# Softcap attention, gated MLP and gated convolution on one core: a new order for the first pairs, a bank moved, the last output in halves

## The chip, the core and the metric

The kernel runs on one core of a Trainium2 chip. Its metric is the device time of one execution in microseconds (us). Several runs are made, and their median counts. One further execution is recorded by the hardware profiler, and that recording is called the trace here.

The core has these engines: TensorE (PE, the matrix multiplies, with PEld for the loading of weights), VectorE (DVE), ScalarE (ACT), GpSimd (POOL) and SyncE (SP, which issues most of the DMAs). Each engine works through its own queue in order. An instruction that waits for a semaphore holds up all that stands behind it on that engine.

## The reference

Three stages follow each other, on 2 batches, 448 positions, 12 heads of 64 and a model width of 768:

```python
scores = scale * q @ k.T                       # per head
scores = cap * tanh(scores / cap)
attn = exp(scores - max); attn /= sum + 1e-9
x = attn @ v                                   # heads laid side by side: [2, 448, 768]

h = gelu(x @ w_in)                             # 768 -> 1024
u, v = h[..., :512], h[..., 512:]
v = layer_norm(v) * g_ln
x = x + (u * (w_sg @ v + b_sg)) @ w_out        # 512 -> 768

h = relu(x @ w2_in)                            # 768 -> 1024
y = (h * sigmoid(conv3(h))) @ w2_out           # 1024 -> 768, the output
```

## The kernel before

**Precision.** Most operands are kept as two parts, hi (rounded) and lo (the rest), and one product is three matmuls: hi by hi, hi by lo, lo by hi. `split` makes the two parts. The weights arrive as 64-bit floats, and `decode` turns each piece into hi and lo with a few ACT and DVE instructions (tiles `f`, `hd`, then `WI`, `WO` or `W`).

**Attention.** The heads are worked on in 12 pairs N, and each pair in two halves, so that the loop in `attention` runs over R = 2N + half. `scores(N, half)` writes scores to the tile `sc`, which takes four PSUM banks and exists once. So the next scores can start only when ACT has read the last ones (`tanh`, L403, into `raw`). ACT then runs `exp` on `raw` in place (L412). Pair 0 is an exception: its first scores go to the tile `pv` instead, and its `tanh` takes the scale `qscale` from a small tile `one`, which `constants` computes from the input `cap`. `one` also holds `guard`, the 1e-9 of the reference under the same shift as the sums.

`value` and `values` then multiply `raw` by the values (`V`, and `vlast` for the last 64 positions) and by ones, which gives the row sums; all this goes to `pv`. For half 0, DVE first adds two key blocks (`sm`, L459), and the sums use `sm`. On ACT `both` is copied to `E` when a pair is complete. Division follows many steps later: sums to `ss`, reciprocal, a round through DRAM to `rb`, then `E` times `rb`, split into `X`. The last pair divides at once through PE (`norm_pe`, with `sel`).

**What sets the order.** PE's order in the attention is written out: each matmul is pinned behind the last one (`ordered`, L386). On ACT and DVE, `pin` does the same for chosen instructions; what is not pinned is placed by a scheduler that plans ahead of the run. `later(k, fn)` puts work k ticks off, two ticks to a step R. SP issues its loads in one pinned order, each waiting for the load eight before it. `IDLE` and `WARM` are matmuls on zeros that keep PE at work.

**Behind the attention.** At R = 23 to 26 four units of the next stage (`FILL`, `mmw`) are computed between the last values. Three of them use the single bank `mo` of the pool `psm`; unit 1 uses a bank of the `sc` tile (`fi`). `gelu` reads such a bank twice, with ACT and DVE alternating, and ends in `u` (L230), which frees the bank. The gated MLP (`u_unit`, `v_unit`, `sg_unit`, `o_unit`) takes its banks by the function `bank`. The last stage ends with `f_unit`: ACT copies 128 by 448 results to `o`, and SP issues the store (L952, L953).

Of the kernel before, what the change touches and what calls it, by code (L numbers as in the profile page):

```python
# [19 lines left out]
P = 128  # L20
# [19 lines left out]

WARM = 15

K0 = 2 * P

IDLE = {0: (1, 4), 3: (3, 5)}

# [7 lines left out]
def stages(  # L54
# [19 lines left out]

    now = [0]
    lasta, lastv, lastr, lasts = [None], [None], [None], [None]

# [55 lines left out]

    heads = []

    def decode_half(hi, lo, src, pool, bufs, wait, hi_eng, top_eng):

        n = src.shape[1]
        r = pool.tile([P, 512, 2], U32, tag="f64", name="f64", bufs=bufs)[:, :n]
        words = r.rearrange("p c w -> p (c w)").bitcast(U16)  # L140
        sync(words[:, : 4 * n - 1], src.rearrange("r c w -> r (c w)").bitcast(U16)[:, 1:])
        low = r[:, :, 0]
        top = words.rearrange("p (c w) -> p c w", w=4)[:, :, 2].bitcast(BF16)
        heads.append(heads.pop(0))
        hd = heads[-1][:, :n]

        def s1():
            half = hd.bitcast(F16).rearrange("p (c w) -> p c w", w=2)[:, :, 1]
            with pin(lasta), pin(lastv):
                if top_eng == "a":  # L150
                    A.activation(half, top, AF.Copy)
                else:
                    V.tensor_copy(half, top)

        def s2():
            V.scalar_tensor_tensor(
                out=low, in0=low, scalar=13, in1=hd, op0=ALU.logical_shift_right, op1=ALU.bitwise_or
            )
            if hi_eng == "a":
                A.activation(hi, f(low), AF.Copy)  # L160
            else:
                V.tensor_copy(hi, f(low))

        def s3():
            V.tensor_tensor(out=lo, in0=f(low), in1=f(hi), op=ALU.subtract)

        for k, fn in zip(wait, (s1, s2, s3)):
            later(k, fn)
# [69 lines left out]
    def u_done(b, i, ps):  # L238
# [7 lines left out]
        later(1, s2b)  # L246

    def constants(pool):
        V.tensor_scalar(
            out=capc, in0=capt, scalar1=CAP_MAX, scalar2=-CAP_MAX, op0=ALU.min, op1=ALU.max  # L250
        )
        V.reciprocal(out=rcap, in_=capc if bounded else capt)
        V.tensor_scalar(
            out=qscale, in0=rcap, scalar1=1.0 / math.sqrt(D), scalar2=None, op0=ALU.mult
        )

        V.tensor_scalar(out=ncap, in0=capc, scalar1=-1.0, scalar2=None, op0=ALU.mult)
        V.tensor_tensor(out=ncap, in0=ncap, in1=capc, op=ALU.min)
        A.activation(guard, ncap, AF.Exp)
        if not bounded:  # L260
            V.tensor_scalar(out=guard, in0=guard, scalar1=1e-9, scalar2=None, op0=ALU.mult)
        heads[:] = [pool.tile([P, 512], U32, name=f"hd{i}") for i in range(2)]
# [12 lines left out]
    def attention(att, psa):  # L275
# [35 lines left out]
        def prep_q(n):  # L311
            qr, _ = qraw[n]
            q = Qt[n] = att.tile([P, 2, S], F32R, tag="Q", name="Q", bufs=2)
            if n == 0:

                A.activation(q[:, 0], qr, AF.Copy)
# [36 lines left out]
        if WARM:  # L353
# [4 lines left out]
            for i in range(WARM):  # L358
                T.matmul(wps, lhsT=wz[:, :P], rhs=wz, start=True, stop=True)  # L359
        constants(att)  # L360
        creg = A.alloc_register("creg")
        A.reg_load(creg, capc[0:1].bitcast(mybir.dt.int32))

# [7 lines left out]
        for t in range(4):  # L371
            G.memset(sel[t * 32 : t * 32 + 1, t], 1.0)
        prep_k(0, slice(0, K0))
        prep_q(0)
        with pin(lastv):
            prep_k(0, slice(K0, ST))
            V.tensor_scalar(out=guard, in0=guard, scalar1=1e-9, scalar2=None, op0=ALU.mult)

# [9 lines left out]

        late, sm0 = [], [None]
        sums = psa.tile([P, 3 * 512], F32, tag="pv", name="pv", bufs=1)  # L390

        def scores(N, half):

# [27 lines left out]
            for g in range(2 * half, 2 * half + 2):  # L421
# [23 lines left out]
                if N == 0 and g < 2:  # L445
                    soft(raw[:, 2 * g : 2 * g + 2], to[:, 2 * g : 2 * g + 2, :S])
                    if g:
                        expo(raw[:, 0:2])
                        expo(raw[:, 2:4])
                if R in IDLE and g == IDLE[R][0]:  # L450
                    for _ in range(IDLE[R][1]):
                        ordered(idle, lhsT=wz[:, :P], rhs=wz, start=True, stop=True)
            if half:
                soft(raw, ps)
            elif N:
                soft(raw, ps[:, :, :S])
            if half == 0:
                held[N] = att.tile([P, 2, S], F32, tag="sm", name="sm", bufs=2)
                sm = V.tensor_tensor(out=held[N], in0=raw[:, 0:2], in1=raw[:, 2:4], op=ALU.add)  # L459
                if N == 0:  # L460
                    sm0[0] = sm

# [119 lines left out]
        def norm_pe(N, both):  # L582

            b, p = divmod(N, NPAIR)
            both_e = att.tile([P, 2 * (S + HS)], F32, tag="E", name="E", bufs=3)[:, S + HS :]
            A.activation(both_e, both, AF.Copy)
            e, r = both_e[:, :S], both_e[:, S:]
            V.tensor_scalar(out=r, in0=r, scalar1=guard, scalar2=None, op0=ALU.add)
            V.reciprocal(out=r, in_=r)

# [16 lines left out]
        for R in range(2 * NN + LAGS[1] + 1):  # L607
            N, half = divmod(R, 2)
            if R == 23:
                columns(att)  # L610
            if R == 4:
                load_vlast(3, NN)
            for j, at in enumerate(WIN):
# [3 lines left out]
            if R < 2 * NN:  # L617
                if half == 0 and N + 2 < NN:
                    load(N + 2)
                if half == 0 and N + 1 < NN:  # L620
                    load_v(N + 1)
                if R == 1:

                    start_values(0)
                    scores(N, half)
                    value(0, 0)
                    value(0, 1)
                else:
                    scores(N, half)
                if R == 2:  # L630
                    values(0, 0, True)
                    done += 1
                if half == 0 and N + 1 < NN:
                    with pin(sm0) if N == 1 else ExitStack():
                        prep_q(N + 1)
                        prep_k(N + 1)
            if R in FILL:

                i, k0, k1 = FILL[R]
                if k0 == 0:  # L640
                    if i == 1:
                        free = psa.tile([P, 4, 512], F32, tag="sc", name="fi", bufs=1)
                    fill[i] = free[:, i, :S] if i == 1 else psm.tile([P, 512], F32, tag="mo", name="mo")[:, :S]
                for k in range(k0, k1):
# [3 lines left out]
            tick()  # L648
            if R > 1 and done < 2 * NN and R - done >= LAGS[R >= LAGS[2]]:
                values(*divmod(done, 2))  # L650
# [77 lines left out]
    def rest():  # L728
# [3 lines left out]
        with ExitStack() as s1:  # L732
# [18 lines left out]
            def bank(n):  # L751
                return (psm if n < 4 or n % 4 == 3 else ps1).tile([P, 512], F32, tag="mo", name="mo")

# [153 lines left out]
        with ExitStack() as s2, ExitStack() as last:  # L907
# [38 lines left out]
            def f_unit(b, m):  # L946
                ps = ps1.tile([P, 512], F32, tag="mo", name="mo")[:, :S]
                c = slice(m * P, (m + 1) * P)
                for i in range(NF):
                    mm3(ps, W2[:, 0, i, c], W2[:, 1, i, c], HG[:, 0, i, b], HG[:, 1, i, b], i == 0, i == NF - 1)  # L950
                o = c2.tile([P, S], F32, tag="cv", name="o", bufs=2)
                A.activation(o, ps, AF.Copy, scale=0.5)  # L952
                nc.sync.dma_start(outT[c, b * S : (b + 1) * S], o)  # L953
# [38 lines left out]
    if bounded:  # L992

        over = one[0:1, 7:8].bitcast(mybir.dt.int32)
        V.tensor_tensor(out=over, in0=capt[0:1], in1=capc[0:1], op=ALU.not_equal)
        flag = nc.values_load(over, min_val=0, max_val=1)
# [70 lines left out]
```

## Time and profile before

| what | value |
| --- | --- |
| median of 3 runs | 327.97 us (326.82 to 328.14) |
| the profiled execution | 327.65 us |
| its span, first to last instruction | 325.8 us |
| mean granted TensorE clock | 0.994 |
| PE busy | 316.0 us |
| PEld busy | 261.6 us |
| DVE busy | 242.7 us |
| ACT busy | 219.8 us |
| POOL busy | 36.7 us |
| DMA | 37.75 MB, mean 116 GB/s |

The span is 1.85 us shorter than the time of the same execution; what lies outside it is start and end. A line number such as L386 is that of the instruction or of the helper which recorded it: all ordered matmuls have L386, so they are told apart by their tiles.

### The profile page before, as it was taken

The page shows a single profiled execution, that of the slowest core. Times are in us where ns is not written, and L with a number is a line of the kernel's source. Part 1 is how long each engine was busy: PE and PEld are TensorE (multiplying, and loading weights), DVE is VectorE, ACT ScalarE, POOL GpSimd, SP SyncE. Part 2 cuts the span into 40 slices and gives each one's busy share as a digit, 9 for nine tenths or more (in the row PEclk, how much of TensorE's full clock was granted, in tenths as well). Part 3 has the DMA queues.
Part 4 walks back from the last instruction along what each step waited for, and adds up shares of the span by engine and source line. Part 5 has one row for each costly group of instructions (what it writes and reads, how often), then busy time and mean ns, then how long its engine had stood idle before and what let it go on. Part 6 is the DMA issues. An engine that isn't in the chain of part 4 may idle for free.

```text
span 325.8 us, 6295 instructions
## 1 busy us (share of the span) xinstructions
PE 316.0 (97%) x2382; PEld 261.6 (80%) x2382; DVE 242.7 (75%) x485; ACT 219.8 (67%) x353; POOL 36.7 (11%) x73
## 2 busy tenths in 40 slices
PE   8998999999999999999999999999999999999992
PEld 6565666666677789988999899999999999999991
DVE  4546998398666899999987979996888999990000
ACT  3998999898973457767565745455777988883010
POOL 4000134051322220211111000000000000000000
PEclk9999999999999999999999999999999999999997
DMA  3488775855423154122213670002391123013211
GB/s 111 117 216 222 243 214 141 222 155 182 156 90 119 58 161 116 52 60 103 66 64 129 198 303 0 2 0 65 112 367 40 32 66 97 1 58 117 84 58 36
DMA packets 22223, 37.75 MB, mean 116 GB/s; under 512 B 7352, under 2 KB 14536, under 8 KB 22184
## 3 DMA queue, kind: packets, MB, share of 16 engines
q1 hardware_dynamic: 20392, 34.51, 34.6%
q0 software_dynamic: 1632, 2.61, 2.7%
q8 instruction: 21, 0.34, 0.4%
q14 instruction: 18, 0.15, 0.2%
q10 hardware_dynamic: 160, 0.13, 0.1%
HBM read 34.40 MB, written 2.79 MB: 114 GB/s over the span
## 4 chain that ended last, share of the span: by engine, by line
PE 70%; DVE 10%; DMA 9%; ACT 6%; issue 2%; SPq 1%; POOL 0%; ACTq 0%; DVEq 0%; POOLq 0%
PE mo L111 14%; PE mo L113 14%; PE mo L112 14%; PE pv L386 11%; PE sc L386 7%; DMA f<-in_w_in_dram 5%; PE mo L386 4%; DMA kr<-in_kT_dram 2%; PE wps L359 1%; ACT raw L403 1%; PE fi L386 1%; PE mo L772 1%; DVE f L191 1%; ACT f L184 1%; PE mo L773 1%
## 5 line engine op out<-in xcount | busy, mean ns | idle before, releaser
L112 PE MATMUL mo<-X,WI 128*128 128x448 f32 x120 | 43.7, 365 | 0.0
L113 PE MATMUL mo<-X,WI 128*128 128x448 f32 x120 | 43.7, 365 | 0.0
L111 PE MATMUL mo<-X,WI 128*128 128x448 f32 x120 | 43.0, 365 | 0.0
L412 ACT ACTIVATE raw<-raw 128x1344 f32<-128x1344 f32 (+2 forms) x25 | 36.4, 1462 | 0.7
L403 ACT ACTIVATE raw<-sc 128x1792 f32<-128x1792 f32 (+1 forms) x22 | 32.4, 1475 | 3.9 <-PE sc L386 3.7
L113 PE MATMUL mo<-HG,W 128*128 128x448 f32 x96 | 34.7, 365 | 0.0
L112 PE MATMUL mo<-HG,W 128*128 128x448 f32 x96 | 34.6, 365 | 0.0
L111 PE MATMUL mo<-HG,W 128*128 128x448 f32 x96 | 33.3, 365 | 0.0
L386 PE MATMUL pv<-raw,V 128*32 128x224 f32 x576 | 32.9, 358 | 0.0
L181 ACT ACTIVATE f<-f 128x256 f32<-128x256 f32 (+2 forms) x44 | 22.8, 517 | 12.9 <-DMA f<-in_w_in_dram 8.1
L191 DVE SCALAR_TENSOR_TENSOR f<-f 128x256 uint32<-128x256 uint32 (+2 forms) x44 | 22.4, 518 | 9.3 <-ACT f L184 8.9
L386 PE MATMUL sc<-Q,K 64*128 64x448 f32 x210 | 27.6, 385 | 0.7 <-ACT raw L403 0.6
L386 PEld LDWEIGHTS pv<-raw,V 128*32 128x32 f32 x576 | 18.8, 109 | 11.5 <-issue 5.5
L386 PEld LDWEIGHTS sc<-Q,K 64*128 64x128 f32 x210 | 18.0, 184 | 10.0 <-ACT raw L403 5.2
L111 PEld LDWEIGHTS mo<-X,WI 128*128 128x128 f32 x120 | 22.5, 188 | 1.9
L112 PEld LDWEIGHTS mo<-X,WI 128*128 128x128 f32 x120 | 22.5, 188 | 1.9
L113 PEld LDWEIGHTS mo<-X,WI 128*128 128x128 f32 x120 | 22.5, 188 | 1.8
L184 ACT ACTIVATE f<-f 128x256 uint32<-128x256 uint32 (+2 forms) x44 | 22.5, 512 | 0.0
L194 DVE SCALAR_TENSOR_TENSOR f<-f 128x256 uint32<-128x256 uint32 (+2 forms) x44 | 22.4, 515 | 0.1
L952 ACT ACTIVATE o<-mo 128x448 f32<-128x448 f32 x12 | 6.3, 542 | 22.8 <-PE mo L113 19.0
L112 PEld LDWEIGHTS mo<-HG,W 128*128 128x128 f32 x96 | 18.0, 188 | 1.4
L111 PEld LDWEIGHTS mo<-HG,W 128*128 128x128 f32 x96 | 18.0, 188 | 1.4
(155 smaller groups left out, 695.5 us busy)
## 6 DMA issues: line engine op xcount, KB each, us to landing
f<-in_w_in_dram SPq DMA_DIRECT2D x12, 512.0 KB, 4.2
f<-in_w_out_dram SPq DMA_DIRECT2D x24, 256.0 KB, 4.8
f<-in_w_in_dram SPq DMA_DIRECT2D x12, 511.8 KB, 5.7
f<-in_w_out_dram SPq DMA_DIRECT2D x8, 384.0 KB, 3.1
qr<-in_qT_dram SPq DMA_DIRECT2D x24, 112.0 KB, 3.0
out_dram<-o SPq DMA_DIRECT2D x12, 224.0 KB, 2.0
rb<-d POOLq DMA_DIRECT2D x22, 112.0 KB, 3.2
V<-in_vL_dram SPq DMA_DIRECT2D x12, 192.0 KB, 3.0
```

Source lines behind the costliest of these rows:

```text
L111: matmul(ps, lhsT=whi, rhs=xhi, start=start, stop=False)
L112: matmul(ps, lhsT=whi, rhs=xlo, start=False, stop=False)
L113: matmul(ps, lhsT=wlo, rhs=xhi, start=False, stop=stop)
L181: A.activation(f(h), f(h), AF.Copy, scale=2.0**-112)
L184: A.activation(l, l, AF.Copy, scale=0.93 * 2.0**-29)
L191: V.scalar_tensor_tensor(out=l, in0=h, scalar=3, in1=l, op0=ALU.logical_shift_left, op1=ALU.bitwise_or)
L194: V.scalar_tensor_tensor(out=l, in0=h, scalar=0x80000000, in1=l, op0=ALU.bitwise_and, op1=ALU.bitwise_or)
L359: T.matmul(wps, lhsT=wz[:, :P], rhs=wz, start=True, stop=True)
L386: lastm[0] = T.matmul(*args, **kw)
L403: lasta[0] = A.activation(x, ps, AF.Tanh, **sc)
L412: lasta[0] = A.activation(x, x, AF.Exp, scale=creg)
L952: A.activation(o, ps, AF.Copy, scale=0.5)
```

## The change

The change has these parts.

1. **The head.** Preparing the first K and Q (`prep_k`, `prep_q`) stands ahead of `constants` on DVE and ACT. `guard` is computed later, by the new function `set_guard`, which is called inside the first scores of pair 1. `WARM` goes from 15 to 13.
2. **Pairs 0 and 1 on PE.** The scores of the second half of pair 1 come ahead of the row sums of the second half of pair 0. The five idle matmuls behind them go, and two stand behind the sums.
3. **DVE and SP.** The preparation of Q and K for pair N+1 is pinned behind the sum `sm` of pair N-1 for every N, no longer for N = 1 alone. `load_vlast(3, NN)`, four loads in rows of 256 bytes, moves from R = 4 to R = 6.
4. **The end of the attention.** Fill unit 3 uses a bank of the `sc` tile, as unit 1 does, and unit 4 of the next stage takes the bank `mo`. In `norm_pe` the copy to `E` is pinned on ACT and the reciprocal is put ahead of a decode step on DVE (`drain`).
5. **The last output.** It is cut in two halves of 224 columns: ACT copies and stores one, DVE copies and SP stores the other.

```diff
-WARM = 15
+WARM = 13
-IDLE = {0: (1, 4), 3: (3, 5)}
+IDLE = {0: (1, 4)}
...
         def s2():
-            V.scalar_tensor_tensor(
+            with pin(drain):
+                V.scalar_tensor_tensor(
...
+    def set_guard():
+        with pin(lastv):
+            V.tensor_scalar(out=ncap, in0=capc, scalar1=-1.0, scalar2=None, op0=ALU.mult)
+        V.tensor_tensor(out=ncap, in0=ncap, in1=capc, op=ALU.min)
+        with pin(lasta):
+            lasta[0] = A.activation(guard, ncap, AF.Exp)
+        guards[0] = V.tensor_scalar(out=guard, in0=guard, scalar1=1e-9, scalar2=None, op0=ALU.mult)
+
     def constants(pool):
...
-        A.activation(guard, ncap, AF.Exp)
...
+        prep_k(0, slice(0, K0))
+        prep_q(0)
         constants(att)
         creg = A.alloc_register("creg")
-        A.reg_load(creg, capc[0:1].bitcast(mybir.dt.int32))
+        with pin(lasta):
+            A.reg_load(creg, capc[0:1].bitcast(mybir.dt.int32))
...
-        prep_k(0, slice(0, K0))
-        prep_q(0)
         with pin(lastv):
             prep_k(0, slice(K0, ST))
-            V.tensor_scalar(out=guard, in0=guard, scalar1=1e-9, scalar2=None, op0=ALU.mult)
...
+                if R == 2 and g == 0:
+                    set_guard()
...
+            if then:
+                then()
...
-                sm = V.tensor_tensor(out=held[N], in0=raw[:, 0:2], in1=raw[:, 2:4], op=ALU.add)
-                if N == 0:
-                    sm0[0] = sm
+                sms[N] = [V.tensor_tensor(out=held[N], in0=raw[:, 0:2], in1=raw[:, 2:4], op=ALU.add)]
...
-            A.activation(both_e, both, AF.Copy)
+            with pin(lasta):
+                lasta[0] = A.activation(both_e, both, AF.Copy)
...
-            V.reciprocal(out=r, in_=r)
+            drain[0] = V.reciprocal(out=r, in_=r)
...
-            if R == 4:
-                load_vlast(3, NN)
...
+                if R == 6:
+                    load_vlast(3, NN)
...
+                elif R == 3:
+
+                    def sums0():
+                        values(0, 1, True)
+                        for _ in range(2):
+                            ordered(idle, lhsT=wz[:, :P], rhs=wz, start=True, stop=True)
+
+                    scores(N, half, sums0)
+                    done += 1
...
                 if R == 2:
                     values(0, 0, True)
+                    value(0, 3)
+                    value(0, 2)
                     done += 1
                 if half == 0 and N + 1 < NN:
-                    with pin(sm0) if N == 1 else ExitStack():
+                    with pin(sms[N - 1]) if N else ExitStack():
...
-                    fill[i] = free[:, i, :S] if i == 1 else psm.tile([P, 512], F32, tag="mo", name="mo")[:, :S]
+                    fill[i] = free[:, i, :S] if i % 2 else psm.tile([P, 512], F32, tag="mo", name="mo")[:, :S]
...
-            if R > 1 and done < 2 * NN and R - done >= LAGS[R >= LAGS[2]]:
+            if R > 2 and done < 2 * NN and R - done >= LAGS[R >= LAGS[2]]:
...
-                return (psm if n < 4 or n % 4 == 3 else ps1).tile([P, 512], F32, tag="mo", name="mo")
+                return (psm if n < 5 or n % 4 == 3 else ps1).tile([P, 512], F32, tag="mo", name="mo")
...
+                if b == B - 1 and m == NK - 1:
+                    A.activation(o[:, :HS], ps[:, :HS], AF.Copy, scale=0.5)
+                    V.tensor_scalar(out=o[:, HS:], in0=ps[:, HS:], scalar1=0.5, scalar2=None, op0=ALU.mult)
+                    nc.scalar.dma_start(outT[c, b * S : b * S + HS], o[:, :HS])
+                    nc.sync.dma_start(outT[c, b * S + HS : (b + 1) * S], o[:, HS:])
+                    return
```

ACT at the very start, with what each instruction waits for (`DMAHW1` and `DMAHW2` are the loads of the two halves of the first `qr`, issued by SP; `one` holds the constants). Before:

```order
L296 DMA kr_89<-in_kT_dram 64x256
L297 DMA kr_89<-in_kT_dram 64x256
L259 ACT_TABLE_LOAD
L259 ACTIVATE one<-one 128x1 [waits DVE_49]
L316 ACTIVATE Q<-qr 128x448 [waits DMAHW2_49,DMAHW1_49]
L403 ACTIVATE raw<-pv,one 128x896 [waits PE_49]
```

And in the changed kernel:

```order
L304 DMA kr_89<-in_kT_dram 64x256
L305 DMA kr_89<-in_kT_dram 64x256
L324 ACT_TABLE_LOAD [waits DMAHW2_49]
L324 ACTIVATE Q<-qr 128x448 [waits DMAHW1_49]
L411 ACTIVATE raw<-pv,one 128x896 [waits DVE_49,PE_49]
L411 ACTIVATE raw<-sc,one 128x896 [waits PE_49]
L373 TENSOR_LOAD one [waits DVE_49]
L420 ACTIVATE raw<-raw 128x896 [waits Activation_49] x2
L411 ACTIVATE raw<-sc,one 128x1344 [waits PE_49]
L420 ACTIVATE raw<-raw 128x1344 [waits Activation_49]
L256 ACTIVATE one<-one 128x1 [waits DVE_49]
L411 ACTIVATE raw<-sc 128x1792 [waits PE_49]
```

The `exp` of `guard` moved from the fourth row to the eleventh, and the copy of Q is now the first activation. The table load stood ahead of every wait; now it stands behind the wait for the second half of `qr`.

PE from the last values of pair 0 to the scores of pair 2 (`K_88` is the K of pair 1, `K_87` that of pair 2). Before:

```order
L386 MATMUL pv<-raw,vlast 64x224 x4
L386 MATMUL pv<-raw,V 32x224 x8
L386 MATMUL pv<-raw,ones_147 32x224 x4
L386 MATMUL pv<-raw,ones_145 32x224
L386 MATMUL pv<-raw,ones_146 32x224
L386 MATMUL pv<-raw,ones_145 32x224
L386 MATMUL pv<-raw,ones_146 32x224
L386 MATMUL sc<-Q,K_88 128x2x224 x6
L386 MATMUL sc<-qr,kl_92 64x224 x4
L386 MATMUL idle<-wz 128x448 x5
L386 MATMUL sc<-Q,K_87 128x448 x12
```

And in the changed kernel:

```order
L394 MATMUL pv<-raw,vlast 64x224 x4
L394 MATMUL pv<-raw,V 32x224 x8
L394 MATMUL sc<-Q,K_88 128x2x224 x6
L394 MATMUL sc<-qr,kl_92 64x224 x4
L394 MATMUL pv<-raw,ones_147 32x224 x4
L394 MATMUL pv<-raw,ones_145 32x224
L394 MATMUL pv<-raw,ones_146 32x224
L394 MATMUL pv<-raw,ones_145 32x224
L394 MATMUL pv<-raw,ones_146 32x224
L394 MATMUL idle<-wz 128x448 x2
L394 MATMUL sc<-Q,K_87 128x448 x12
```

The scores of pair 1's second half moved ahead of eight instructions with ones.

DVE from the sum of pair 1 to that of pair 2 (`sm_262` and `sm_347` before, `sm_260` and `sm_338` in the changed kernel; `K1_88` is the K of pair 3, `K0_87` that of pair 4, `f64` and `hd0` a weight piece under decoding). Before:

```order
L459 TENSOR_TENSOR sm_262<-raw_247 128x896
L105 CAST K1_88<-kr1_90 128x384
L320 TENSOR_SCALAR Q_349<-qr_238,one_72 128x448
L108 TENSOR_TENSOR K1_88<-kr1_90,K1_88 128x384
L153 CAST hd0_139<-f64_296 128x512
L335 TENSOR_SCALAR kl1_92<-kr1_90,one_72 128x64
L321 SCALAR_TENSOR_TENSOR Q_349<-qr_238,one_72,Q_349 128x448
L156 SCALAR_TENSOR_TENSOR f64_296<-f64_296,hd0_139 128x512
L162 CAST WI0_76<-f64_296 128x512
L165 TENSOR_TENSOR WI0_76<-f64_296,WI0_76 128x512
L105 CAST K0_87<-kr0_89 128x384
L459 TENSOR_TENSOR sm_347<-raw_332 128x896
```

And in the changed kernel:

```order
L471 TENSOR_TENSOR sm_260<-raw_241 128x896
L328 TENSOR_SCALAR Q_340<-qr_232,one_72 128x448
L106 CAST K1_88<-kr1_90 128x384
L343 TENSOR_SCALAR kl1_92<-kr1_90,one_72 128x64
L329 SCALAR_TENSOR_TENSOR Q_340<-qr_232,one_72,Q_340 128x448
L109 TENSOR_TENSOR K1_88<-kr1_90,K1_88 128x384
L155 CAST hd0_139<-f64_284 128x512
L159 SCALAR_TENSOR_TENSOR f64_284<-f64_284,hd0_139 128x512
L165 CAST WI0_76<-f64_284 128x512
L168 TENSOR_TENSOR WI0_76<-f64_284,WI0_76 128x512
L471 TENSOR_TENSOR sm_338<-raw_323 128x896
```

The cast of pair 4's K, which stood ahead of the sum of pair 2, now stands behind it.

## Rows read from the trace of the kernel before

**Rows 1.** Stretches: start:end, length, busy (x count) by engine, PEclk, DMA share, GB/s.
```profile
19.20:31.00 11.80, 10.84 (x160) 7.11 (x162) 6.60 (x13) 11.52 (x9) 1.30 (x2) 1.00 0.88 218
31.00:45.00 14.00, 14.00 (x218) 9.34 (x216) 12.52 (x27) 12.30 (x10) 3.78 (x7) 1.00 0.75 216
150.00:185.00 35.00, 34.92 (x170) 31.37 (x169) 30.35 (x57) 22.71 (x39) 3.38 (x4) 1.00 0.34 106
```

**Rows 2.** Timeline, PE: start, us, engine, line, what [idle before <-releaser].
```profile
1.38 4.80 PE L359 MATMUL wps<-wz 128*128 128x448 f32 x15 [1.38 <-DVE wz L356]
...
6.11 1.06 PE L386 MATMUL pv<-Q,K 64*128 64x448 f32 x6
...
15.47 0.96 PE L386 MATMUL pv<-raw,ones 128*32 128x224 f32 x16
...
19.18 1.49 PE L386 MATMUL sc<-Q,K 64*128 64x448 f32 x12 [0.19 <-ACT raw L403]
...
30.20 0.58 PE L386 MATMUL pv<-sm,ones 128*32 128x224 f32 x8 [0.96 <-DVE sm L459]
...
38.83 0.56 PE L386 MATMUL pv<-raw,vlast 64*64 64x224 f32 x8
...
106.58 3.94 PE L386 MATMUL mo<-X,WI 128*128 128x448 f32 x18 [0.40 <-DVE u L230]
```

**Rows 3.** Timeline, ACT and the issue queues of ACT and SP, 0 to 33 us.
```profile
0.73 0.56 ACTq L296 DMA_DIRECT2D kr<-in_kT_dram  x1
0.73 1.46 SPq L85 DMA_DIRECT2D qr<-in_qT_dram  x2
...
1.96 1.28 ACT L259 ACT_TABLE_LOAD   x1 [1.96 <-issue]
...
5.20 0.20 ACT L259 ACTIVATE one<-one 128x1 f32<-128x1 f32 x1 [1.96 <-DVE one L258]
5.35 0.58 ACT L316 ACTIVATE Q<-qr 128x448 fp32r<-128x448 f32 x1
...
7.22 1.01 ACT L403 ACTIVATE raw<-pv,one 128x896 f32<-128x896 f32 x1 [1.29 <-PE pv L386]
...
13.75 1.66 ACT L403 ACTIVATE raw<-sc 128x1792 f32<-128x1792 f32 x1 [0.32 <-PE sc L386]
...
17.83 1.30 ACT L403 ACTIVATE raw<-sc 128x1344 f32<-128x1344 f32 x1 [0.69 <-PE sc L386]
...
19.47 2.69 SPq L85 DMA_DIRECT2D vlast<-in_vL_dram  x4
...
31.34 0.53 SPq L85 DMA_DIRECT2D V<-in_vL_dram  x1
...
32.20 1.29 ACT L403 ACTIVATE raw<-sc 128x1344 f32<-128x1344 f32 x1 [1.21 <-PE sc L386]
```

**Rows 4.** DMA issues by line: count, KB each, median us to landing.
```profile
qr<-in_qT_dram SPq DMA_DIRECT2D x24, 112.0 KB, 3.0
vlast<-in_vL_dram SPq DMA_DIRECT2D x4, 144.0 KB, 5.2
...
kr<-in_kT_dram ACTq DMA_DIRECT2D x2, 64.0 KB, 3.4
```

**Rows 5.** Timeline, DVE.
```profile
28.78 0.36 DVE L105 CAST K<-kr 128x384 fp32r<-128x384 f32 x1 [1.91 <-DMA kr<-in_kT_dram]
29.06 1.08 DVE L459 TENSOR_TENSOR sm<-raw 128x896 f32<-128x896 f32 x1
```

**Rows 6.** Waits of PE's weight loads, 112 us to the end: total, times, longest.
```profile
PEld mo L111 <- DVE gt L823: 0.5, 1, 0.5
```

**Rows 7.** Timeline of the end, ACT and SP's queue.
```profile
319.64 0.54 ACT L952 ACTIVATE o<-mo 128x448 f32<-128x448 f32 x1 [4.32 <-PE mo L113]
320.21 0.33 SPq L953 DMA_DIRECT2D out_dram<-o  x1
```

**Rows 8.** A stretch behind the last store's issue, columns as in rows 1.
```profile
322.00:325.80 3.80, 0.00 (x0) 0.00 (x0) 0.00 (x0) 0.00 (x0) 0.00 (x0) 0.52 0.03 9
```

More of the change, by code (lines that the diff above doesn't have):

```diff
@@ L75, in stages @@
     now = [0]
+    guards = [None]
     lasta, lastv, lastr, lasts = [None], [None], [None], [None]
@@ L134, in stages @@
     heads = []
+    drain = [None]
     def decode_half(hi, lo, src, pool, bufs, wait, hi_eng, top_eng):
@@ L155, in s2 @@
         def s2():
-            V.scalar_tensor_tensor(
-                out=low, in0=low, scalar=13, in1=hd, op0=ALU.logical_shift_right, op1=ALU.bitwise_or
-            )
+            with pin(drain):
+                V.scalar_tensor_tensor(
+                    out=low, in0=low, scalar=13, in1=hd, op0=ALU.logical_shift_right, op1=ALU.bitwise_or
+                )
             if hi_eng == "a":
@@ L246, in u_done @@
         later(1, s2b)
+    def set_guard():
[5 more added lines that the diff above has]
+        guards[0] = V.tensor_scalar(out=guard, in0=guard, scalar1=1e-9, scalar2=None, op0=ALU.mult)
     def constants(pool):
-        V.tensor_scalar(
-            out=capc, in0=capt, scalar1=CAP_MAX, scalar2=-CAP_MAX, op0=ALU.min, op1=ALU.max
-        )
+        with pin(lastv):
+            V.tensor_scalar(
+                out=capc, in0=capt, scalar1=CAP_MAX, scalar2=-CAP_MAX, op0=ALU.min, op1=ALU.max
+            )
         V.reciprocal(out=rcap, in_=capc if bounded else capt)
-        V.tensor_scalar(
+        lastv[0] = V.tensor_scalar(
             out=qscale, in0=rcap, scalar1=1.0 / math.sqrt(D), scalar2=None, op0=ALU.mult
         )
-        V.tensor_scalar(out=ncap, in0=capc, scalar1=-1.0, scalar2=None, op0=ALU.mult)
-        V.tensor_tensor(out=ncap, in0=ncap, in1=capc, op=ALU.min)
-        A.activation(guard, ncap, AF.Exp)
         if not bounded:
-            V.tensor_scalar(out=guard, in0=guard, scalar1=1e-9, scalar2=None, op0=ALU.mult)
+            set_guard()
         heads[:] = [pool.tile([P, 512], U32, name=f"hd{i}") for i in range(2)]
@@ L314, in prep_q @@
             if n == 0:
-                A.activation(q[:, 0], qr, AF.Copy)
+                lasta[0] = A.activation(q[:, 0], qr, AF.Copy)
                 with pin(lastv):
@@ L372, in attention @@
             G.memset(sel[t * 32 : t * 32 + 1, t], 1.0)
-        prep_k(0, slice(0, K0))
-        prep_q(0)
         with pin(lastv):
             prep_k(0, slice(K0, ST))
-            V.tensor_scalar(out=guard, in0=guard, scalar1=1e-9, scalar2=None, op0=ALU.mult)
         raws, acc, held, pairs = {}, {}, {}, []
@@ L386, in ordered, with scores @@
                 lastm[0] = T.matmul(*args, **kw)
-        late, sm0 = [], [None]
+        late, sms = [], {}
         sums = psa.tile([P, 3 * 512], F32, tag="pv", name="pv", bufs=1)
-        def scores(N, half):
+        def scores(N, half, then=None):
             R = 2 * N + half
@@ L449, in scores @@
                         expo(raw[:, 2:4])
+                if R == 2 and g == 0:
+                    set_guard()
                 if R in IDLE and g == IDLE[R][0]:
@@ L994, in stages @@
         over = one[0:1, 7:8].bitcast(mybir.dt.int32)
-        V.tensor_tensor(out=over, in0=capt[0:1], in1=capc[0:1], op=ALU.not_equal)
+        with pin(guards):
+            V.tensor_tensor(out=over, in0=capt[0:1], in1=capc[0:1], op=ALU.not_equal)
         flag = nc.values_load(over, min_val=0, max_val=1)
```

## Prediction

> **What bounds the kernel.** I read the table of busy times first: PE is busy 316.0 of 325.8 us, far ahead of the rest. So the places where PE stands still come next, and for them the table of stretches and PE's timeline. From 31 us on PE has no gap in the attention (14.00 of 14.00 us busy, [rows 1]); behind that it waits 0.40 us at the fourth fill unit [rows 2] and 0.5 us for `gt` in the gated MLP [rows 6]. Ahead of 31 us it is otherwise: between 19.2 and 31 PE is busy 10.84 of 11.80 us and ACT 11.52 [rows 1]. ACT's own timeline shows why. From the first `tanh` at 7.22 its `tanh` and `exp` follow each other, and it waits for PE only 0.32, 0.69 and 1.21 us at the three places shown [rows 3]. So ACT bounds the head, PE all the rest, and nothing but the head, the fill units, the gated MLP and the last store can move the time. The sum is made against the profiled execution, 327.65 us (span 325.8, and 1.85 around it); the median stands 0.32 above it.
>
> **Term 1, the first Q: +1.1 us.** The order of ACT shows what the timeline alone would not: the table load, 1.28 us, ran at 1.96, ahead of every wait and while ACT had nothing else to do [rows 3]. In the changed order it stands behind the wait for the second half of the first `qr`, since the copy of Q is now the first activation and has two waits. That half is SP's second issue, so it is issued at about 0.73 + 1.46 / 2 = 1.46 [rows 3]. No row gives its own landing. With the 3.4 us of the `kr` loads issued at the same time [rows 4] it lands at 4.86 (with the 3.0 of the median `qr`, earlier); it had landed when Q was copied, at 5.35 [rows 3]. Behind it come 1.28 us of table load, so the copy starts between 6.14 and 6.63 in place of 5.35: +0.8 to +1.3. I take +1.1, a little above the middle, since the copy began as soon as the `exp` ahead of it let it, and nothing shows that the load had long been there. Against this the change lets Q go ahead of the `exp` of `guard` (5.20 to 5.35, [rows 3]), which is 0.15 us and is in these figures already. The first `tanh` waited for PE's first scores and these for Q, so the whole chain on ACT moves by the term. PE's 13 warm-up matmuls of 4.80 / 15 = 0.32 us end at about 1.38 + 4.16 = 5.5, the first scores start at 6.11 + 1.1 = 7.2 [rows 2]: a hole of up to 1.7 us. The later `exp` of `guard` (0.20) stands ahead of a `tanh` that waited 0.32 for PE [rows 3], so it is free.
>
> **Term 2, scores ahead of sums: -0.66 us.** The `tanh` at 17.83 waited 0.69 us for the scores of the second half of pair 1 [rows 3]; ahead of those PE ran the 16 matmuls with ones, 0.96 us [rows 2], which now come behind. 0.96 is more than 0.69, so the wait goes, and ACT, which bounds this stretch, starts earlier by all of it but a handover of about 0.03. The sums run later while ACT works; if they come to be waited for by the copy out of `pv`, the gain could shrink to half.
>
> **Term 3, `sm` of pair 2: -0.96 us.** PE waited 0.96 us for `sm` at 30.20 [rows 2]. DVE had been idle 1.91 us, up to 28.78, for a `kr` load; the cast of K ran first and `sm` from 29.06 to 30.14 [rows 5]. The cast now stands behind `sm`. Then `sm` can start when DVE comes free, 28.78 - 1.91 = 26.87, or when `raw` is ready, and with its 1.08 us it ends at 28 or soon after, while PE asks at 30.20 - 0.96 = 29.24. The wait goes whole. The cast runs 1.1 us later than it could, but it makes the K of pair 4, which is wanted two pairs on. The next thing late is ACT's `tanh` at 32.20, which waited 1.21 us for PE [rows 3]: ACT has that much to give, so the gain is not lost there.
>
> **Term 4, `vlast`: 0.** Four issues of 2.69 us on SP's queue, at 19.47, go behind the V that was issued at 31.34 [rows 3], and what stood behind them on SP (`qr`, `kr`, V) comes up to 2.69 us sooner. The four then are issued from 31.34 + 0.53 = 31.87, or up to 2.69 sooner, and the last one starts about 2 us on. With 3.0 (a `qr`) to 5.2 us (an earlier `vlast` load, [rows 4]) to land, that is between 34.2 and 39.1. The values of pair 3 read `vlast` at 38.83 [rows 2], a little earlier with terms 2 and 3. So the cost is 0 unless all comes late, and then some 0.5 to 1. I take 0; the drop in DMA load between 19 and 31 us (share 0.88, [rows 1]) could bring as much.
>
> **Term 5, the fourth fill unit: -0.40 us.** It waited 0.40 us because unit 2 still held the one bank `mo` until `u` was done [rows 2]. With a bank of `sc`, free since the last `tanh`, the wait goes. The other moves there, the copy to `E` and the reciprocal put ahead, shorten a chain that PE did not wait for.
>
> **Term 6, the gated MLP: +0.4 us.** Here DVE is busy 30.35 of 35 us, and PE meets it once, at `gt` (0.5 us, [rows 1, 6]). PE would arrive there earlier by some 0.8 us (terms 3 and 5 and what is left of 1 and 2); DVE follows only in part, since its decode steps keep their own pace. Its order is also a new one. Bounds: 0, if the whole DVE chain moves along, and +1.0, if PE's lead is lost altogether. I take +0.4.
>
> **Term 7, the last output: -0.15 us.** Half a copy saves up to half of 0.54 [rows 7], less a fixed part: about 0.2, and the two halves run at the same time on ACT and DVE. But ACT's queue takes 0.56 us for an issue [rows 3] where SP's takes 0.33 [rows 7], and the later half sets the end: 0.23 more if ACT's store is the later one, and two stores under way at once can hinder each other. On the other side each moves half the bytes, which can save some more. So the bounds are -0.4 and +0.2; I take -0.15, nearer the saving of the copy, since the first store need not be the later one to land.
>
> **Sum.** 1.1 - 0.66 - 0.96 - 0.40 + 0.4 - 0.15 = -0.67: 326.98 for a profiled execution, and a median of 327.3 us. The parts add up in this way because the shift of ACT in the head is carried through to the fill units (PE has no gap in between to take it up), and terms 2 and 3 are taken off the same path.
>
> **Rivals.** A difference under 0.5%, 1.64 us, can't be told from no change here; faster means below 326.33, slower above 329.61.
>
> *The first Q is not late.* If the table load still runs in the idle time at the start, the copy starts at 5.20, when the `exp` of `guard` did, and the change does in full what its order says: 327.3 - 1.1 - 0.15 = 326.0, down to 325.6 if term 6 costs nothing. For it: ACT was idle until 1.96 and the load needs no data. Against it: in the trace the load ran in its place in the order, behind ACT's two issues. Chance 0.23 (0.21 faster, 0.02 same).
>
> *TensorE's clock falls in the new hole.* The granted clock is 1.00 in all the stretches of rows 1, where the longest idle time is 0.96, and 0.52 in the stretch behind the last work [rows 8], that is near the lower level, 1.2 of 2.4 GHz. A hole of 1.7 us at the start lies between. If it falls there, the first scores (1.06), those of one further half (1.49) and the sums (0.96, [rows 2]) run at double time on the path that feeds ACT: +3.5, or 330.8 us. This is the case on the other side, and it decides as soon as the first scores take near 2 us in place of 1.06. Against it: the hole is short beside the 3.8 us of rows 8. Chance 0.11 (0.10 slower).
>
> *DVE takes back more in the gated MLP.* With +1.0 or a little over in term 6, and `vlast` late by 0.5, the gains are gone: 328.1 to 328.4. Chance 0.10, nearly all the same.
>
> *Something follows the table load.* ACT idled 1.96 us between the load's end, 3.24, and 5.20, which is put down to DVE's `one` [rows 3]; a tail of the load of up to that length would not have shown. Behind the wait it would: up to 327.3 + 1.96 = 329.3, and some more with bad terms. Chance 0.06 (0.02 slower, 0.04 same). The Trainium skill, in "ScalarE: Activation LUTs", section "What ACT_TABLE_LOAD costs", names 1283 ns for the load, with which the trace's 1.28 agrees, and a drain of 1380 ns behind it, which no row here shows; by that page the time would be some 1.4 us above my sum, an estimate of 328.7.
>
> The forecast itself keeps 0.50, of which 0.07 lies below 326.33. Together: faster 0.28, same 0.59, slower 0.13. The range goes from 325.5, just below the first rival's good end, to 329.4, which leaves out the fallen clock; its own range for the likeliest case is 326.2 to 328.4.
>
> **What would show it.** In the trace of the changed kernel: the table load near 4.9 to 5.3 in place of 1.96, the copy of Q behind it, the first scores near 7.2 (term 1; if the load stands near 2, the first rival holds); no wait for PE at the `tanh` of pair 1's second half (term 2); no wait of PE for `sm` near 30 and the cast of K behind it (term 3); `vlast` landed before PE asks near 38 (term 4); no wait at the fourth fill unit (term 5); PE's waits for `gt` at 150 to 185 near 0.9 in place of 0.5 (term 6); the last two issues on ACT and SP and the span's end behind them (term 7). A granted clock under 1.00 between 5 and 20 us would show the second rival. The prediction is wrong in its mechanism if the load is not late, or if PE waits for something after 31 us that it did not wait for before.

## The result and the profile after

The changed kernel takes 330.89 us (median of 5 runs, 330.15 to 331.11) against 327.97. The ratio is 1.0093, 95% interval 1.0074 to 1.0113: slower by 2.9 us, above the forecast of 327.3 and above its range. The profiled execution has a span of 329.3 us (325.8 before).

The attention went better than forecast. First comes the timeline of the changed kernel (PE, ACT, SP; columns as in rows 2), at the places of terms 1 to 5:

```profile
1.38 5.22 PE L367 MATMUL wps<-wz 128*128 128x448 f32 x13 [1.38 <-DVE wz L364]
...
4.98 1.28 ACT L324 ACT_TABLE_LOAD   x1 [4.98 <-DMA qr<-in_qT_dram]
6.28 0.58 ACT L324 ACTIVATE Q<-qr 128x448 fp32r<-128x448 f32 x1
...
6.91 1.14 PE L394 MATMUL pv<-Q,K 64*128 64x448 f32 x6 [0.31 <-ACT Q L324]
...
8.08 1.01 ACT L411 ACTIVATE raw<-pv,one 128x896 f32<-128x896 f32 x1 [1.23 <-PE pv L394]
...
17.96 1.29 ACT L411 ACTIVATE raw<-sc 128x1344 f32<-128x1344 f32 x1
...
28.79 3.29 SPq L86 DMA_DIRECT2D vlast<-in_vL_dram  x4
...
29.15 0.60 PE L394 MATMUL pv<-sm,ones 128*32 128x224 f32 x8
...
37.79 0.56 PE L394 MATMUL pv<-raw,vlast 64*64 64x224 f32 x8
...
105.07 3.94 PE L394 MATMUL fi<-X,WI 128*128 128x448 f32 x18
```

Against rows 2 and 3: the table load waits for `qr` and the first `tanh` comes 0.86 us later than before; the `tanh` of pair 1's second half waits for nothing and is only 0.13 late; the sums of pair 2 wait for nothing and are 1.05 ahead; `vlast` is not waited for; the fourth fill unit starts 1.51 us ahead. So at the end of the attention the change had gained 1.5 us.

All of it and three more were lost behind the attention. This is the table of stretches of the kernel before, from the gated MLP on (columns as in rows 1; the second number with its count is the weight loads):

```profile
112.00:150.00 38.00, 38.00 (x177) 32.82 (x176) 36.43 (x70) 25.42 (x50) 6.04 (x7) 1.00 0.31 91
150.00:190.00 40.00, 39.92 (x194) 35.99 (x193) 35.31 (x66) 25.53 (x44) 3.38 (x4) 1.00 0.41 133
262.00:300.00 38.00, 38.00 (x189) 35.22 (x189) 30.27 (x71) 29.09 (x75) 0.00 (x0) 1.00 0.20 68
```

And of the changed kernel, with the stretch of rows 1 ahead of 31 us, where PE now has no gap:

```profile
19.20:31.00 11.80, 11.80 (x177) 7.97 (x180) 8.14 (x17) 11.54 (x10) 1.30 (x2) 1.00 0.83 226
...
112.00:150.00 38.00, 38.00 (x180) 32.56 (x177) 34.37 (x65) 23.80 (x48) 8.32 (x6) 1.00 0.30 91
150.00:190.00 40.00, 38.63 (x183) 33.41 (x182) 35.05 (x67) 25.12 (x44) 3.66 (x4) 1.00 0.40 128
262.00:300.00 38.00, 37.05 (x181) 33.44 (x180) 32.88 (x78) 30.90 (x79) 0.00 (x0) 1.00 0.18 60
```

Read the weight loads: from 150 to 190 PE does 182 in place of 193, from 262 to 300 180 in place of 189. At the usual 0.203 us from one to the next that is 2.2 + 1.8 = 4.0 us. Ahead of that, from 112 to 150, PE still keeps pace, but DVE does 34.37 us of work in place of 36.43: DVE falls behind by 2.1 us before PE has to wait for it. The waits of PE's weight loads from 112 us on, in the changed kernel (columns as in rows 6, which is the one wait before):

```profile
PEld mo L113 <- DVE gl L109: 2.8, 4, 0.8
PEld mo L112 <- ACT HG L108: 1.3, 1, 1.3
PEld mo L112 <- ACT VN L822: 0.3, 1, 0.3
PEld mo L794 <- DVE E L578: 0.3, 1, 0.3
PEld mo L112 <- DVE gt L845: 0.2, 1, 0.2
PEld mo L112 <- ACT GH L108: 0.2, 1, 0.2
```

Where DVE stood still is seen in the timeline of ACT and DVE near 147 us. In the changed kernel:

```profile
143.69 0.54 ACT L201 ACTIVATE WO<-f 128x384 fp32r<-128x384 f32 x1
147.10 1.09 ACT L226 ACTIVATE gs<-mo 128x512 f32<-128x512 f32 x2 [2.88 <-PE mo L796]
...
145.26 0.54 DVE L206 TENSOR_TENSOR WO<-f,WO 128x384 fp32r<-128x384 f32 x1
147.73 1.28 DVE L229 SCALAR_TENSOR_TENSOR gs<-gs,mo 128x512 f32<-128x512 f32 x2 [1.93 <-ACT gs L226]
```

And before:

```profile
142.89 0.60 ACT L223 ACTIVATE gs<-mo 128x512 f32<-128x512 f32 x1 [1.00 <-PE mo L774]
148.93 0.60 ACT L223 ACTIVATE gs<-mo 128x512 f32<-128x512 f32 x1 [1.33 <-DVE VN L801]
```

In the changed kernel ACT waits 2.88 us for PE and then takes two V units (`gs`) at once; DVE waits 1.93 behind it. Before, ACT took those units 6 us apart, and no wait of DVE between 140 and 152 was longer than 0.48. The reason stands in the orders of PE and ACT. Before, the unit of the last 64 positions (`WI,GH`) was done whole and first, and the last three V units came after it, one by one: 18, 54 matmuls. In the changed order 26 matmuls of two of these units stand ahead of it and 28 behind: 26, 18, 28. The first of these two units has all its 18 matmuls by 141.2, but ACT's queue still has the unit of the last 64 positions ahead of it, and PE ends that one at 147.1. So ACT stands still with a finished unit at hand, and DVE, which has the most to do after PE in this stage, runs dry.

### The profile page after: what moved, and what is told of

The parts are those of the page before. It is cut to its first block, busy times and chain, and to the rows that moved or that the text cites. A ratio compares the mean times of both kernels' runs of the same rounds, so it can differ in the third digit from the quotient of the medians.

```text
span 329.3 us, 6282 instructions
## 1 busy us (share of the span) xinstructions
PE 318.2 (97%) x2377; PEld 260.7 (79%) x2377; DVE 244.3 (74%) x486; ACT 219.6 (67%) x353; POOL 39.1 (12%) x73
## 4 chain that ended last, share of the span: by engine, by line
PE 71%; DVE 9%; ACT 8%; DMA 7%; issue 2%; SPq 1%; ACTq 0%; DVEq 0%
PE pv L394 16%; PE mo L113 11%; PE mo L112 11%; PE mo L114 11%; PE sc L394 10%; DMA f<-in_w_in_dram 4%; PE mo L394 2%; DMA f<-in_w_out_dram 2%; PE fi L394 2%; PE mo L794 2%; PE mo L795 2%; PE mo L796 2%; ACT f L187 2%; ACT f L184 1%; DVE f L194 1%
## 5 line engine op out<-in xcount | busy, mean ns | idle before, releaser
L194 DVE SCALAR_TENSOR_TENSOR f<-f 128x256 uint32<-128x256 uint32 (+2 forms) x44 | 22.9, 531 | 10.4 <-ACT f L187 10.1
L197 DVE SCALAR_TENSOR_TENSOR f<-f 128x256 uint32<-128x256 uint32 (+2 forms) x44 | 22.9, 527 | 0.2
```

The costliest lines, as they stand in the source:

```text
L194: V.scalar_tensor_tensor(out=l, in0=h, scalar=3, in1=l, op0=ALU.logical_shift_left, op1=ALU.bitwise_or)
L197: V.scalar_tensor_tensor(out=l, in0=h, scalar=0x80000000, in1=l, op0=ALU.bitwise_and, op1=ALU.bitwise_or)
```

## The experiments

Ratios are to the kernel before, run beside each set on the same chip. Experiments 1 to 4, 5 to 8 and 9 to 12 are three sets on three chips, where it took 327.89, 327.67 and 327.78 us; between sets the ratios compare better than the times. In the first kernels one part of the change is put back.

**1. Both bank edits put back.**

```diff
-fill[i] = free[:, i, :S] if i % 2 else psm.tile(...)
+fill[i] = free[:, i, :S] if i == 1 else psm.tile(...)
-return (psm if n < 5 or n % 4 == 3 else ps1).tile(...)
+return (psm if n < 4 or n % 4 == 3 else ps1).tile(...)
```

> The changed kernel with one thing put back: fill unit 3 uses the bank mo again and unit 4 of the next stage the other pool. PE's order behind the attention is then that of the kernel before; all of the head and the last output stay as changed. Theory A (the new order of the gated MLP's units, which came with the banks, cost the time: PE was 1.5 us ahead at the fourth fill unit and lost 4.6 us behind it): about 327.0 us, 1.1 us ahead at the end of the attention less some 0.1 to 0.4. Theory B (PE comes too early for DVE and ACT, whatever the order): 329 to 331, with waits of PE for gl near 165 and 185 and for HG near 272.

326.93 us, ratio 0.9961 (0.9936 to 0.9986). The table of stretches has PE without a gap again and DVE's work where it was:

```profile
112.00:150.00 38.00, 38.00 (x176) 32.82 (x176) 36.79 (x71) 25.03 (x50) 6.70 (x7) 1.00 0.31 91
150.00:190.00 40.00, 40.00 (x196) 36.45 (x195) 35.71 (x67) 25.64 (x45) 2.75 (x3) 1.00 0.43 141
262.00:300.00 38.00, 38.00 (x189) 35.22 (x188) 28.36 (x68) 28.83 (x73) 0.00 (x0) 1.00 0.20 69
```

PE comes to the fourth fill unit at 105.80, 0.78 ahead of before, and the span is 0.7 shorter: the lead is kept, so theory B falls. It even grows, to 1.29 at PE's last matmul, since the wait for `gt` [rows 6] is gone too.

**2. The kernel before with the two bank edits alone** (the lines of experiment 1 the other way round).

> The kernel before with only the two bank edits of part 4 (fill unit 3 in the bank of sc, unit 4 of the next stage in mo). Theory A (order): 330 to 332 us, since the 4.6 us are lost without the head's gain of 1.1; PE's waits for gl and HG are there. Theory B (PE too early): about 327.6, since PE's lead is only the 0.40 of the fill unit.

331.70 us, ratio 1.0132 (1.0091 to 1.0173). ACT waits for the two V units as in the changed kernel, and PE for `HG` and `VN` (timeline of ACT and waits of PE's weight loads):

```profile
148.16 1.09 ACT L223 ACTIVATE gs<-mo 128x512 f32<-128x512 f32 x2 [2.85 <-PE mo L774]
```

```profile
PEld mo L111 <- ACT HG L107: 1.6, 1, 1.6
PEld mo L111 <- ACT VN L800: 1.5, 1, 1.5
PEld mo L112 <- DVE gl L108: 1.1, 2, 0.8
```

Experiments 1 and 2 together: the two bank edits cost about 4 us (330.89 - 326.93, and 331.70 - 327.89), the rest of the change gains about 1.

**3. An early table load**, the rest as changed.

```diff
             V.memset(f(wz), 0.0)
+            A.activation(ncap, f(wz)[:, 0:1], AF.Exp)
```

> The changed kernel with a one-column exp of a zeroed tile as ACT's first activation, so that the table load runs in the idle time at the start; all other orders are the same. The first Q should be copied at about 5.0 in place of 6.28 and the first tanh come near 7.0 (8.08 in the changed kernel). Theory A (what PE loses in the gated MLP does not depend on its lead): 330.9 - 1.0 = 329.9. Theory B (DVE sets the pace there, and a lead is given back): 330.7 to 331.

329.79 us, ratio 1.0078 (1.0047 to 1.0109). ACT at the start:

```profile
2.25 1.28 ACT L365 ACT_TABLE_LOAD   x1 [2.25 <-issue]
...
4.95 0.58 ACT L324 ACTIVATE Q<-qr 128x448 fp32r<-128x448 f32 x1 [1.21 <-DMA qr<-in_qT_dram]
...
7.52 1.01 ACT L412 ACTIVATE raw<-pv,one 128x896 f32<-128x896 f32 x1 [1.99 <-PE pv L395]
```

Q is copied 1.33 us sooner, but the first `tanh` only 0.56 sooner: the scores now wait for PE to finish its warm-up matmuls. The median is 1.1 lower, but it is of another set; by the ratios it is 0.5, near the 0.56 of the head.

**4. Banks put back and early table load.**

> The banks put back as in the first run and the early table load of the third, together. Theory A: 326.0 us, the first run's time less 1.0. Theory B: no better than the changed kernel.

326.44 us, ratio 0.9955 (0.9933 to 0.9977), 0.49 below the first run. So an early load is worth about 0.5, where term 1 had priced the late one at 1.1.

**5. Only unit 4's pool put back** (`n < 4`; fill unit 3 stays in the bank of `sc`).

> The changed kernel with the pool of unit 4 put back (n < 4) and fill unit 3 left in the bank of sc. The planner then keeps the V unit of the last 64 positions (18 matmuls with WI, GH) ahead of the 53 matmuls of the last three V units, nearly as in the kernel before; in the changed kernel it stands between them (26, 18, 28). Theory A1 (the loss comes from the V units interleaved in this way: ACT waits 2.9 us for two results at once near 147 and DVE 1.9 behind it): 326.5 to 327, as fast as with both edits back, or 0.4 faster. Theory A2 (the loss comes from PE running ahead without the wait at the fourth fill unit): 330 or more.

327.90 us, ratio 0.9984 (0.9956 to 1.0013). The V units stand as before (18, 53), the waits for `gl` are gone, and 3 of the 4 us with them. A wait for `HG` of 0.5 us is left, and one wait is new, right behind the fill units:

```profile
112.40 0.50 PE L794 MATMUL mo<-WI,X 128*128 128x512 f32 x1 [1.26 <-DVE u L233]
```

The 0.40 us that the fourth fill unit no longer waits for DVE's `u` come back as 1.26 for the next `u`, one unit on: that `u` reads `fi` from 111.73 to 112.35, and unit 4 takes a bank of the four that `fi` holds. The bank had been moved, not DVE made faster.

**6. Only the fill unit put back** (unit 4 stays in `mo`).

> The changed kernel with fill unit 3 back in mo and the pool of unit 4 left as changed (n < 5). The V unit of the last 64 positions stays between the others (22, 18, 32). Theory A1: 330 to 331, slower than before, with the 0.40 wait at the fourth fill unit as well and waits for gl near 165. Theory A2: about 327.

330.94 us, ratio 1.0091 (1.0060 to 1.0121): as slow as the whole change. V units 22, 18, 32, and DVE waits again:

```profile
147.43 1.28 DVE L229 SCALAR_TENSOR_TENSOR gs<-gs,mo 128x512 f32<-128x512 f32 x2 [1.77 <-ACT gs L226]
```

So the one edit `n < 5` is enough for the whole loss.

**7. The first run without the pins behind `sm`.**

```diff
-                    with pin(sms[N - 1]) if N else ExitStack():
+                    with pin(sms[0]) if N == 1 else ExitStack():
```

> The first run's kernel (banks put back) without the pin of K and Q behind sm for all pairs but the first; the order behind the attention is the same. My term 3: PE waits again 0.96 us for sm of pair 2, so about 326.9 + 0.9 = 327.8. Rival: the earlier loads that the moved vlast allows land before the cast needs them, the wait shrinks on its own, and the time stays at 327.0.

327.52 us, ratio 0.9975 (0.9948 to 1.0003). The intervals of this and the first run overlap. The trace shows that the wait did not come back:

```profile
29.23 0.60 PE L394 MATMUL pv<-sm,ones 128*32 128x224 f32 x8
```

and the fourth fill unit starts at 105.90 against 105.80. SP's queue shows why: the `kr` loads that stood behind `vlast` are issued 3.1 us sooner. First before, then in this run:

```profile
24.61 2.40 SPq L85 DMA_DIRECT2D kr<-in_kT_dram  x3
21.49 1.82 SPq L86 DMA_DIRECT2D kr<-in_kT_dram  x3
```

The cast of K runs ahead of `sm` again, at 26.00, but no longer waits. So the 0.96 us go without the pin. Whether the pin alone, without the move, would also take them away was not run.

**8. The first run with PE's order of pairs 0 and 1 as before** (sums ahead of scores, five idle matmuls).

```diff
-IDLE = {0: (1, 4)}
+IDLE = {0: (1, 4), 3: (3, 5)}
...
-                elif R == 3:
-                    scores(N, half, sums0)
...
```

> The first run's kernel (banks put back) with PE's order of pairs 0 and 1 as before: sums ahead of the scores of pair 1's second half, five idle matmuls, none after. PE's order behind the attention is the same. My term 2: the tanh of those scores waits 0.69 us again and the time is about 326.9 + 0.66 = 327.6. Rival: the shift is taken up by ACT's later waits for PE, and the time stays at 327.0.

327.76 us, ratio 0.9987 (0.9961 to 1.0014), 0.83 above the first run; the fourth fill unit starts at 106.64 against 105.80, which is 0.84. ACT's wait is back as it was:

```profile
19.00 1.29 ACT L411 ACTIVATE raw<-sc 128x1344 f32<-128x1344 f32 x1 [0.70 <-PE sc L394]
```

In this trace PE's hole ahead of the first scores is longer than in the changed kernel, and the granted clock (the 1.00 in the second row) does not fall:

```profile
7.18 1.14 PE L394 MATMUL pv<-Q,K 64*128 64x448 f32 x6 [1.30 <-ACT Q L324]
5.00:20.00 15.00, 13.33 (x146) 7.96 (x144) 8.93 (x25) 12.50 (x12) 0.26 (x1) 1.00 0.49 134
```

**9. The changed kernel with the V units' order pinned**, both bank edits kept.

```diff
+                    with pin(lastu if t > 3 and k == 0 else [None]):
                         T.matmul(ps, lhsT=xs(0, k), rhs=WI[1][:, 0, k], ...)
...
+                    lastu[0] = T.matmul(ps, lhsT=xs(1, k), rhs=WI[1][:, 0, k], ...)
```

> The changed kernel as it is, both bank edits included, with one pin more on PE: the first matmul of each of the last three V units is pinned behind the last matmul of the unit ahead of it. PE then runs the 18 matmuls of the last 64 positions whole and first, and the other 54 one unit after the other (in the changed kernel 26, 18, 28). Theory A1 (the interleaved V units cost the time): 326.5 us, since the wait at the fourth fill unit stays away; up to 327.9 if a new wait for a bank comes, as in the fifth run. Rival (the banks themselves, by when DVE frees them, cost the time): 329.5 or more.

328.24 us, ratio 1.0020 (0.9997 to 1.0043): 2.65 less than the changed kernel (2.4 by the ratios), by one order on PE. DVE's wait near 147 is 0.61 in place of 1.93, its work from 112 to 150 is 35.83 us in place of 34.37, and PE's waits for `gl` and `HG` are gone. What is left is one long wait, shown by PE's timeline:

```profile
138.78 0.47 PE L797 MATMUL mo<-WI,GH 128*128 128x512 f32 x1 [1.36 <-DVE u L233]
```

This explains the planner. Behind the attention there is a ring of seven banks, and beside it the one bank `mo`. In both kernels `bank` gives `mo` to unit 7, the first of the four units that follow the first three V units, and then to unit 11, that of the last 64 positions. With `n < 5` unit 4 has it ahead of them. The planner then puts unit 7 behind 42 matmuls of its neighbours, where it stood first; its `u`, which frees `mo`, comes at 137.68 in the changed kernel against 133.41 before; and unit 11 would have to wait. Without the pin the planner filled that wait of 1.36 us with 26 matmuls of the next units, 5.9 us, and so cost DVE its work. My expectation had 326.5 to 327.9; the 1.36 us are a little more than I had allowed.

**10. The ninth with the early table load.**

> The ninth run's kernel with the early table load of the third. Theory A1: 0.5 to 1.0 us less than the ninth, 325.5 to 326. Rival (DVE sets the pace behind the attention): no less than the ninth.

327.67 us, ratio 0.9995 (0.9972 to 1.0017): 0.57 less than the ninth, the size of the head's step once more, though 1.7 above my upper figure, since the wait of the ninth is in it.

**11. The fourth with the last output whole.**

```diff
-                if b == B - 1 and m == NK - 1:
-                    A.activation(o[:, :HS], ps[:, :HS], AF.Copy, scale=0.5)
-                    V.tensor_scalar(out=o[:, HS:], in0=ps[:, HS:], ...)
-                    nc.scalar.dma_start(...)
-                    nc.sync.dma_start(...)
-                    return
```

> The fourth run's kernel (banks put back, early table load) with the last output whole again: one copy on ACT, one store by SP. PE's order is the same. My term 7: 0.15 us slower, 326.6. Rival: ACT's slower issue and the second store eat the saving, and it is the same or up to 0.2 faster; the tail from PE's last matmul to the end of the span tells it.

325.87 us, ratio 0.9950 (0.9934 to 0.9966), the fastest of all and 1.9 below the kernel before. It is 0.57 below the fourth, which is of another set; the ratios are 0.0005 apart and their intervals overlap, so the times alone don't decide. The traces do: from PE's last start to the end of the span the three with a whole last output (before, experiments 2 and 11) have 6.44 to 6.60 us, the eleven with halves 7.01 to 7.53. The timeline of the end, first of the fourth (halves), PE, ACT, DVE and the queues:

```profile
317.15 0.37 PE L114 MATMUL mo<-HG,W 128*128 128x448 f32 x1
317.60 0.36 ACT L976 ACTIVATE o<-mo 128x224 f32<-128x224 f32 x1 [4.32 <-PE mo L114]
317.99 0.36 ACTq L978 DMA_DIRECT2D out_dram<-o  x1
317.99 0.39 DVE L977 TENSOR_SCALAR o<-mo 128x224 f32<-128x224 f32 x1 [27.82 <-ACT o L976]
318.41 0.33 SPq L979 DMA_DIRECT2D out_dram<-o  x1
```

and of the eleventh (whole):

```profile
316.76 0.37 PE L114 MATMUL mo<-HG,W 128*128 128x448 f32 x1
317.22 0.54 ACT L975 ACTIVATE o<-mo 128x448 f32<-128x448 f32 x1 [4.32 <-PE mo L114]
317.79 0.33 SPq L976 DMA_DIRECT2D out_dram<-o  x1
```

DVE's half does not run beside ACT's: it waits for ACT's copy into the same tile `o` (the releaser of its row), so the last store is issued 1.26 us after PE's last start with halves and 1.03 with one piece. From there to the end of the span it is 6.2 and 5.4 us; why two stores end later than one is open. Two tiles for the two halves were not run. (DVE's order changes a little with this edit as well, PE's does not.)

**12. The changed kernel again.**

> The changed kernel once more, for one look. In its first trace PE's matmuls started every 207 ns from 272 us on, behind the wait for HG, where all other stretches and the traces without that wait show 202 to 203. If the wait brings the slower pace, it is there again; if it is a thing of single executions, the pace is 203 and the span about 1 us shorter, 328.3.

One run of 329.85, span 328.1, with the waits of the first trace (`gl` 2.4, `HG` 1.2) and a pace of 203 behind them. So the slower pace isn't a consequence of the wait that comes each time.

## Why the prediction was wrong

**The step that failed is term 6**: "the gated MLP: +0.4 us ... Bounds: 0, if the whole DVE chain moves along, and +1.0, if PE's lead is lost altogether." PE's lead of 1.51 at the fourth fill unit is a lag of 3.1 at its last matmul (322.28 against 319.19): this term is +4.6, for the gated MLP and the stage behind it, which the prediction had left out and where PE waits for `HG`. Some 0.9 of it is the slower pace told of at the end; in the second trace of the same kernel (experiment 12) a lead of 1.23 becomes a lag of 1.86, which is 3.1. I bounded the term by PE's lead, as if the worst were to give the lead back. That is not what happened: in the old order PE keeps its whole lead (experiment 1, 0.78 at the fourth fill unit and 1.29 at the last matmul).

The sentence "Its order is also a new one" had no price, and the order is what cost the time. Experiments 1, 2, 5, 6 and 9 show it: about 4 us come and go with the banks, `n < 5` alone is enough for them, and some 2.5 of them go when only the order of four V units is put right. How DVE's 2 us near 147 become PE's waits for `gl` and then for `HG` was not followed step by step; that both go with the order is what experiment 9 shows. DVE's 30.35 of 35 us of work [rows 1] left it little room to catch up, and PE's new order, which could be read ahead of any run, had the V units taken apart. My rival on this stage had the right place, but its mechanism was the lost lead, and its size a third or less. By the sign that I had named, PE waiting behind 31 us for something that it did not wait for before, the mechanism was wrong.

**Term 1** (+1.1): the mechanism was right. Q started 0.93 later and the first `tanh` 0.86 [rows 3]; in the other seven traces with the late load that `tanh` is 0.84 to 1.22 late.

But an early load gives back only about 0.5 by the medians (experiments 4 and 10), since the first scores also wait for the warm-up to end. I had that end at 5.5, from the mean of before, 0.32 us a matmul. That mean mixes two paces. Before, the warm-up matmuls behind the first start 0.373 us apart up to 4.53 us and 0.20 apart from 4.81 on; in the changed kernel they start 0.373 apart to the end of the 13, at 6.60. For 448 columns 0.373 us is TensorE's lower level, 1.2 GHz. (The clock column reads 1.00 there too, but the trace has no record of the granted clock ahead of 7.14 us, 4.68 before.) In the traces with 13 matmuls the warm-up ends anywhere between 5.85 and 6.61, as the faster pace comes earlier or later or not at all. So the hole on PE was 0.31 us in the first trace, not 1.7, and 1.30 at most (experiment 8); there the granted clock stays at 1.00 from 5 to 20 us, so the rival of the fallen clock did not come true.

The copy of Q starts 1.30 us after the table load's start, right behind its 1.28: the rival of something that follows the load falls. The Trainium skill, "ScalarE: Activation LUTs", section "What ACT_TABLE_LOAD costs", has a drain of 1380 ns behind the load for a switch to another set of functions; this trace, with its one load, does not show it, and the measurement decides.

**Term 2** (-0.66): -0.73 in the trace (0.86 late at the first `tanh`, 0.13 at that of pair 1's second half), and 0.83 by experiment 8. Right.

**Terms 3 and 4** (-0.96 and 0): the wait went, and `vlast` was in time. But by experiment 7 the gain needs no pin: with `vlast` moved, which I had at 0, the `kr` loads are issued 3.1 us sooner, and DVE does not wait for them [rows 5]. Whether the pin, the reason that I gave, would do it alone is not shown.

**Term 5** (-0.40): the wait at the fourth fill unit went. But nothing made DVE's `u` earlier, and the next unit that wants a bank pays: 1.26 us in experiment 5. The edit `n < 5` keeps that unit out of the bank and moves the wait on along `mo`: 1.36 in experiment 9. With the wait left in place (experiments 1, 4 and 11) there is no other. I had asked what is late next at term 3, and did not ask it here.

**Term 7** (-0.15): +0.45 by the tail of the profiles (from PE's last start to the end of the span 6.59 before, 7.04 changed); over all traces the tails with halves are 0.4 to 1.1 longer (experiment 11). I had let the two halves "run at the same time on ACT and DVE"; they ran one after the other. The sign was wrong, and the size was beyond my bound of +0.2.

## What to carry to other kernels

A wait for a buffer that is taken away by giving another buffer moves to the next user of that one, unless the engine that frees it gets faster; look for that user in the changed order. Where the second engine is busy 30 of 35 us, as DVE was here, a pause of 2 us on it was followed by 3 to 4 us of waits of PE, so price a new order by the longest wait that it gives to that engine, not by the lead of the bound one. When one engine's order changes, see whether the engine behind it still takes the results in the old order, as ACT did. And split a last output only if the two halves really run side by side: the trace's releaser of the second half tells it.

## What the runs showed of the hardware that I had not expected

In the first trace of the changed kernel PE's matmuls start every 0.203 us up to the wait for `HG`, and every 0.207 from there to the end. In PE's stretches (busy time and count of PE, granted clock, DMA share, GB/s):

```profile
200.00:260.00 60.00, 60.00 (x297) 1.00 0.24 80
276.00:318.00 42.00, 42.00 (x205) 1.00 0.19 71
```

In the second trace of the same kernel (experiment 12) the latter stretch holds four matmuls more:

```profile
276.00:318.00 42.00, 42.00 (x209) 1.00 0.19 69
```

Over 240 matmuls that is about 1 us, at the same granted clock of 1.00. Of the six traces with a wait for `HG` two have it (this and experiment 5, where the wait was 0.5), four do not (experiments 2, 3, 6 and 12, waits of 0.9 to 1.6), and none of the eight traces without such a wait has it. So it can begin with a pause of PE, but the length of the pause does not decide it. What does is open; the 4 us of the banks do not rest on it, since experiments 2 and 6 have them without it.
